# Chunked attention and top-1 experts on one core: PSUM banks of their own, loads beside the attention, a last round that leaves old slots in place

## The chip, the cores and the metric

The kernel runs on one core of a Trainium2 chip. The core has TensorE (PE: matrix products, and transposes by a product with the identity), VectorE (DVE), ScalarE (ACT), GpSimd (POOL), and SyncE (SP), which here only issues transfers. Sixteen DMA engines move data between the device memory (HBM) and the on-chip memory (SBUF). TensorE writes into PSUM, whose banks are read by VectorE and ScalarE. The metric is the device time of one execution in microseconds: 314.8 us for the kernel before, the median of three runs between 313.82 and 316.25.

## The reference

Two blocks in a row. The first is attention in chunks: 4 batches, 8 heads, 768 tokens, head dimension 64. A chunk of 32 queries sees 8 memory keys of its head and the keys from 16 before the chunk to 8 after it.

```python
scores = scale * np.matmul(q_c, k_full.transpose(0, 1, 3, 2))
a = np.exp(scores - np.max(scores, axis=-1, keepdims=True))
a = a / (np.sum(a, axis=-1, keepdims=True) + 1e-09)
out[:, :, c_start:c_end] = np.matmul(a, v_full)
```

The result, as 3072 tokens of 512 numbers, goes into eight experts. Each token goes to the one expert with the largest logit, and an expert keeps at most 80 tokens, those with the largest gate weight. A token that is kept becomes its gate weight times the expert's output; the others stay zero.

```python
logits = x @ w_gate                      # 3072 x 8
expert_idx = np.argmax(logits, axis=1)   # gate_w: its softmax probability
keep = np.argpartition(-gw, capacity)[:capacity]
h = np.maximum(x[tok_idx] @ w1[e], 0.0)  # 512 -> 1024
out[tok_idx] = gate_w[tok_idx, None] * (h @ w2[e])
```

All is in float32. One w1 or w2 matrix has 2.1 MB, and there are sixteen.

## The kernel before, in words

**Attention units.** The attention is cut into 32 units: a pair of heads, and half of a sequence (384 tokens). Four units make a round, which has all 512 features of 384 tokens; there are eight rounds. The loop over `i` (line 763) issues for each unit: `scores(i + 1)`, eight products in float32 on a mask product and two exponentials on ScalarE; the turns of a later k or q (`turn_k`, `turn_q`: GpSimd copies the loaded block into another order, TensorE transposes it, VectorE or ScalarE copies the result out of PSUM into `kT` or `qT`); `turn_x(i - 1)`, the transposes of the unit before's output; `values(i)` with `divide` on VectorE. It then issues the loads of k, q and v for later units. v's load is issued two units ahead, in rows of 64 numbers.

**Routing.** The class `Ranks` keeps a table of the best 80 tokens of each expert and merges each round into it. Its ten `steps` are spread over the four units of the next round, two in each unit, through the deque `later`. They weigh x with the gate matrix (`weigh`, `logits`), pick the expert (`gates`), count for each token how many of the round's tokens are ahead of it (`count`, `sum_counts`, `turn_counts`), compare it with the table's tokens (`rivals`, `older`), give everyone a slot (`slots`), and build the new table by products with one-hot matrices (`fill`). In `older`, the matrix `hoto` says which slot each old token moves to. The last round's steps have no later units to lie in: they follow the attention one by one (lines 810 to 843), and `place` makes from their result the token numbers that the gathers need.

**PSUM.** Four pools: `ps_t` with two buffers, shared by the turns of k and q, the turns of x and all steps of `Ranks`; `ps_s` with three for scores; `ps_o` with two for values; `ps_l` with one for the gate products.

**Experts.** `run_experts` gathers the 80 rows of an expert, turns them, multiplies with w1 (`up`, hidden tile hT), with w2 (`down`), turns back, scales and scatters the rows to the output. Nine matrices fit at once (`WR = 9`). w0, w1, the third (w2, in the tile `ld` that the q and k loads use until then), w3 and w4 have places of their own; w5 to w8 take the room of the attention's tiles. A later matrix is loaded by `load_next` in four pieces of 512 KB as soon as the one in its place has been used, and each piece waits until the third before it has landed. `busy` issues products of zeros that only keep TensorE working.

**The order of the transfers.** Nearly all are issued by SP, one after another, in the order of the program, and a transfer that waits for a buffer holds those behind it. The deque `slow` holds pieces that are not urgent: w0 and w1 in eight pieces, then `ld` in four. In the loop one is issued at every third unit from the ninth, and one at each of the last six. After the loop come w3 and w4, each whole, twelve transfers of zeros to the output (512 KB each), and w5 to w8, each whole. `in_order` fixes each engine's order as written.

Of the kernel before, what the change touches and what calls it, by code (L numbers as in the profile page):

```python
# [12 lines left out]
F32 = mybir.dt.float32  # L13
BF16 = mybir.dt.bfloat16
# [48 lines left out]
def kernel(  # L63
# [58 lines left out]
    behind = const.tile([128, 128 * (2 * NT - 1)], BF16, name="behind")  # L122
    iot = const.tile([128, cap], BF16, name="iot")
    iop = const.tile([cap, 1], F32, name="iop")
    idx_g = const.tile([cap, E], I32, name="idx_g")
# [24 lines left out]
    def busy(out, n, cols=DM // 2):  # L150

        for _ in range(n):
            nc.tensor.matmul(
                out[:, :cols], lhsT=zero[:, :128], rhs=zero[:, :cols], start=True, stop=True,
                skip_group_check=True,
            )

    class Weights:
# [32 lines left out]
    class Attention:  # L191
# [83 lines left out]

        def turn_q(self, n):
            if n >= NP:
                return
            qT = self.qT[n] = self.io.tile([128, S], F32, name="qT", tag="qT", bufs=5)

            qh = self.io.tile([NC, T0, 2, D], F32, name="qh", tag="turn", bufs=1)
            nc.gpsimd.tensor_copy(  # L282
                qh.rearrange("p t e d -> p e t d"), self.qs[n].rearrange("p e (t d) -> p e t d", d=D)
            )
            for t0 in range(0, T0, 4):
                pt = self.ps_t.tile([128, 4, NC], F32, name="pq", tag="t")
                for t in range(4):
                    nc.tensor.transpose(  # L288
                        pt[:, t, :], qh[:, t0 + t].rearrange("p e d -> p (e d)"), ident[:NC, :NC]
                    )  # L290
                nc.scalar.copy(  # L291
                    qT.rearrange("p (x t) -> p x t", t=T0)[:, :, t0 : t0 + 4], pt.rearrange("p t x -> p x t")
                )
# [75 lines left out]
    class Ranks:  # L369
# [3 lines left out]
        def __init__(self, gt, ps_t):  # L373
# [7 lines left out]
                mores=([32 * NT, HT], BF16), own=(full, F32), ahead=([128, NT], F32), slot=([128, NT], BF16),  # L381
                hot=([128, NT, cap], BF16), tab=([cap, ND, E], BF16), tabT=([3 * E, cap], BF16),
            )
# [92 lines left out]

        def older(self):

            over = self.ps("over")
            for i in range(NT):  # L480
                nc.tensor.matmul(
                    over[:cap, :E], lhsT=self.older_[:, i, :], rhs=self.oh[:, i, 0, :],
                    start=i == 0, stop=i == NT - 1,
                )
            nc.vector.tensor_reduce(self.beaten, self.older_, axis=AX, op=Alu.add)

# [86 lines left out]
        def steps(self, r, xTs, lu):  # L573
# [21 lines left out]
            ]  # L595

        def place(self, acc):

# [40 lines left out]
    with ExitStack() as actx:  # L639
        ps_t = actx.enter_context(tc.tile_pool(name="ps_t", bufs=2, space=PSUM))  # L640
        ps_s = actx.enter_context(tc.tile_pool(name="ps_s", bufs=3, space=PSUM))
        ps_o = actx.enter_context(tc.tile_pool(name="ps_o", bufs=2, space=PSUM))
        ps_l = actx.enter_context(tc.tile_pool(name="ps_l", bufs=1, space=PSUM))
        at = Attention(actx, ps_t, W.given[WR0])
# [36 lines left out]
        def for_slots():  # L681
            iot_i = gt.tile([128, cap], I32, name="iot_i")
            nc.gpsimd.iota(iot_i, pattern=[[1, cap]], base=1, channel_multiplier=0)
            nc.gpsimd.tensor_copy(iot, iot_i)
            iop_i = gt.tile([cap, 1], I32, name="iop_i")
            nc.gpsimd.iota(iop_i, pattern=[[0, 1]], base=1, channel_multiplier=1)
# [4 lines left out]

        slow = deque()
        for i in range(WR0):
            slow += W.load(i, 4)
        units = [(HP * b + c, f) for b in range(B) for f in range(2) for c in range(HP)]
        P, o, xr, xTs, lus = {}, {}, {}, {}, {}
# [31 lines left out]
        def turn_x(i):  # L728
            xTs[i] = at.turn_x(i, xr[i // HP], ps_t.tile([128, 512], F32, name="xt", tag="t"))

# [16 lines left out]
        later, done = deque(), deque()  # L747
        ranks = Ranks(gt, ps_t)
        start = len(list(nc.cur_bb.bb.instructions))
        busy(ps_o.tile([128, 512], F32, name="oy", tag="o"), 8)  # L750
        at.turn_k(0, nc.vector.tensor_copy)
        at.turn_q(0)
        at.turn_mem()
        at.put_mk(0)
        at.load_k(2)
# [7 lines left out]
        for i in range(NU):  # L763
# [4 lines left out]
            for kind, m in turns.get(i, []):  # L768
                (at.turn_k if kind == "k" else at.turn_q)(m)
            if i:  # L770
                turn_x(i - 1)
            if i in constants:
                constants[i]()
            if later:
                later.popleft()()
            values(i)
            if i and i % HP == 0:
                lus[r] = ps_l.tile([128, 512], F32, name="lu", tag="l")
                steps = ranks.steps(r - 1, [xTs[i - HP + c] for c in range(HP)], lus[r])
# [4 lines left out]
            if later:  # L784
                later.popleft()()
            for kind, m in turns.get(i, []):
                (at.load_k if kind == "k" else at.load_q)(m + 2)
# [6 lines left out]
            if i == NU - 6:  # L794
                slow += W.load(WR0, 4)
            if i >= NU - 6 or i >= 8 and i % 3 == 0:
                if slow:
                    slow.popleft()()
        turn_x(NU - 1)
        at.store(NR - 1, xr[NR - 1])  # L800
        for dma in slow:
            dma()
        for i in range(WR0 + 1, WR0 + 1 + WR2):
            for dma in W.load(i):
                dma()
        for dma in zeros():
            dma()


        r = NR - 1  # L810
        lp = ps_l.tile([128, 512], F32, name="lp", tag="l")

        nc.tensor.matmul(lp[:, : NT * E], lhsT=zerob, rhs=zerob[:, : NT * E], start=True, stop=False)
        early(range(HP - 1), lp)
        later.popleft()()
# [14 lines left out]
        for i in range(NT):  # L830
# [8 lines left out]
            if i == 1:  # L839
                ranks.older()  # L840
        ranks.slots(r, more)
        ranks.place(ranks.fill(r))
        busy(wait, 5)
        judge()
        in_order(start)

    def run_experts(ectx, tag, W, verdict=None, read_flag=None):
# [25 lines left out]

        pieces = deque()

        def load_next(i):

            if i < 2 * E:
                for dma in W.load(i, 4):
                    dma()  # L880
                    pieces.append(list(nc.cur_bb.bb.instructions)[-1])
                    if len(pieces) > 3:
                        tc.add_manual_dep(pieces[-1], pieces.popleft().name, follow, reason="pieces")

# [83 lines left out]
        turn_in(0)  # L968
        busy(ps_h.tile([128, 4 * cap], F32, name="wait", tag="hp"), 4)
        up(0)  # L970
# [17 lines left out]
    with ExitStack() as fctx:  # L988
        fw = fctx.enter_context(tc.tile_pool(name="fw", bufs=1, reuse_waits="tile"))
        W.pools[WR0 + 1 + WR2 :] = [fw] * (WR - WR0 - 1 - WR2)  # L990
        for i in range(WR0 + 1 + WR2, WR):
            for dma in W.load(i):
                dma()
        run_experts(fctx, "", W, verdict, read_flag)

    with tc.If(redo[1] > 0):  # L996

        with ExitStack() as actx:
# [12 lines left out]
            for i, (n, f) in enumerate((HP * b + c, f) for b in range(B) for f in range(2) for c in range(HP)):  # L1011
# [43 lines left out]
                if c == HP - 1:  # L1055
                    at.store(r, xr)
                    steps = ranks.steps(r, xTs, ps_l.tile([128, 512], F32, name="lu2", tag="l"))
                    for step in steps[: None if r < NR - 1 else 8]:
                        step()
            ranks.place(ranks.fill(NR - 1))  # L1060
        with ExitStack() as fctx:
# [34 lines left out]
```

## Time and profile before

The parts of the span (313.2 us), each row an answer of the trace for that stretch, times in us:

| stretch | what lies in it | PE busy | DVE | ACT | POOL | matmul clock | DMA share | GB/s |
|---|---|---|---|---|---|---|---|---|
| 0 to 20 | start, first units | 16.66 | 3.78 | 4.66 | 9.69 | 1.00, then 0.68 | 0.85, then 1.11 | 201, 232 |
| 20 to 60 | attention | 35.34 | 19.30 | 17.68 | 21.83 | 0.95 | 0.92 | 207 |
| 60 to 100 | attention | 35.19 | 20.27 | 18.13 | 17.62 | 0.91 | 0.83 | 184 |
| 100 to 140 | attention | 36.02 | 18.43 | 16.51 | 14.47 | 0.83 | 0.70 | 163 |
| 140 to 160 | attention | 17.45 | 10.92 | 8.94 | 5.32 | 1.00 | 0.68 | 170 |
| 220 to 240 | experts | 15.44 | 3.07 | 1.75 | 1.92 | 0.97 | 1.00 | 361 |
| 240 to 260 | experts | 19.10 | 2.17 | 1.31 | 3.80 | 0.94 | 0.97 | 309 |
| 260 to 280 | experts | 15.46 | 2.77 | 1.31 | 0.94 | 0.83 | 0.91 | 309 |

How to read it: "busy" counts each matmul from its start to its modelled end, so a busy TensorE is not one at its peak; the clock is the share of full speed granted to it. The DMA share is the time of the packets over 16 engines' time, and it can pass 1 since packets overlap; the GB/s beside it say what these packets carried. Over the whole span TensorE is busy 83%, VectorE 33%, ScalarE 26%, GpSimd 28%, and 70.44 MB move. The page's chain of work that ended last covers only the final scatters, so the stages have to be read from their own stretches.

In what follows, "unit 5" is the unit whose exponentials start at 37.77 us, unit 21 starts at 120.96 and unit 31 at 168.26. The last values product of the attention ends near 174, the first expert matmul starts at 200.39, and the last transpose of the experts ends near 301.5.

### The profile page before, as it was taken

How to read it: one execution, taken by the hardware profiler on the slowest of the kernel's cores; microseconds unless marked ns; L12 is line 12 of the kernel's file. 1: busy time of each engine (PE TensorE's matmuls, PEld its weight loads, DVE VectorE, ACT ScalarE, POOL GpSimd, SP SyncE). 2: the span in 40 equal slices, each digit the busy share in tenths (PEclk: the TensorE clock that was granted, in tenths of full speed). 3: DMA queues.
4: the chain of work that ended last, by engine and by line, in shares of the span. 5: the costliest groups of instructions: out<-in, count | busy, mean ns of one | idle time of the engine just before them, and what ended most of it. 6: DMA issues, size and time to landing. Idle time of an engine off the chain costs nothing. (4 is left out here: it accounts for less than half of the span.)

```text
span 313.2 us, 11255 instructions
## 1 busy us (share of the span) xinstructions
PE 258.4 (83%) x4982; PEld 219.8 (70%) x4982; DVE 103.3 (33%) x281; ACT 81.0 (26%) x196; POOL 88.1 (28%) x207
## 2 busy tenths in 40 slices
PE   8798898899889898888897777897797999499940
PEld 6677776677576776766775755786786988398830
DVE  1314337336366247264364364001101011010220
ACT  1234445424444334354454110010100101011000
POOL 3557518153173144260411013110012021010210
PEclk9859999969999759799999655799997999789985
DMA  7999995957959965817858499999998999993010
GB/s 190 230 229 222 195 228 121 268 122 160 270 119 284 226 152 152 180 36 211 197 153 277 138 378 390 375 322 365 395 386 278 349 279 305 307 312 117 25 38 16
DMA packets 63239, 70.44 MB, mean 225 GB/s; under 512 B 34621, under 2 KB 40797, under 8 KB 63181
## 3 DMA queue, kind: packets, MB, share of 16 engines
q1 hardware_dynamic: 61165, 66.65, 75.9%
q0 software_dynamic: 1056, 2.62, 2.4%
q8 instruction: 41, 0.67, 0.9%
q10 hardware_dynamic: 960, 0.36, 0.6%
q14 instruction: 17, 0.14, 0.2%
HBM read 55.72 MB, written 13.89 MB: 222 GB/s over the span
## 5 line engine op out<-in xcount | busy, mean ns | idle before, releaser
L897 PE MATMUL hp<-xn,w 128*64 128x80 f32 x896 | 37.0, 243 | 10.1 <-DMA w<-in_moe_w_dram 5.8
L897 PEld LDWEIGHTS hp<-xn,w 128*64 128x64 f32 x896 | 34.8, 145 | 12.3 <-DMA w<-in_moe_w_dram 6.6
L719 ACT ACTIVATE P<-sp 128x384 f32<-128x384 f32 x64 | 27.9, 488 | 44.3 <-PE sp L711 44.3
L711 PEld LDWEIGHTS sp<-qT,kT 64*128 64x128 f32 x512 | 36.7, 208 | 1.2 <-POOL kT L296 0.7
L711 PE MATMUL sp<-qT,kT 64*128 64x96 f32 x512 | 36.8, 289 | 0.5 <-POOL kT L296 0.4
L911 PE MATMUL yt<-hT,w 128*64 128x80 f32 x896 | 34.6, 239 | 0.9 <-issue 0.9
L911 PEld LDWEIGHTS yt<-hT,w 128*64 128x64 f32 x896 | 33.2, 142 | 2.4 <-issue 2.3
L901 ACT ACTIVATE hT<-hp 128x320 f32<-128x320 f32 x16 | 7.0, 437 | 98.0 <-PE hp L897 98.0
L333 PE MATMUL o<-vw,P 128*32 128x65 f32 x1536 | 32.1, 235 | 0.0
L959 POOL DMA_INDIRECT out_dram<-y,idx_s x7 | 6.5, 930 | 80.1 <-DVE y L958 60.6
L351 PE MATMUL xt<-ident,xr 128*128 128x128 f32 x96 | 18.4, 304 | 12.2 <-ACT qT L291 5.0
L322 DVE COPY kT<-pk 128x480 f32<-128x480 f32 x32 | 19.9, 654 | 24.0 <-PE pk L317 24.0
L333 PEld LDWEIGHTS o<-vw,P 128*32 128x32 f32 x1536 | 26.5, 117 | 1.4 <-issue 0.5
L429 POOL TENSOR_TENSOR desc<-oh,masks 128x24 bf16<-128x24 bf16 x16 | 3.3, 225 | 70.8 <-DVE over_s L340 34.7
L351 PEld LDWEIGHTS xt<-ident,xr 128*128 128x128 f32 x96 | 10.5, 147 | 17.6 <-ACT qT L291 6.9
L872 DVE COPY xn<-xp 128x320 f32<-128x320 f32 x8 | 3.9, 492 | 55.3 <-PE xp L870 55.3
L233 POOL COPY vw<-mv 8x512 f32<-8x512 f32 x32 | 20.0, 626 | 2.9 <-DMA mv<-in_mem_v_dram 2.9
L353 ACT COPY xT<-xt 128x384 f32<-128x384 f32 x32 | 15.4, 480 | 17.6 <-PE xt L351 17.5
L305 POOL COPY kh<-ld 96x1024 f32<-96x1024 f32 x15 | 15.5, 1033 | 12.5 <-issue 8.2
L282 POOL COPY qh<-ld 96x1024 f32<-96x1024 f32 x16 | 16.6, 1036 | 8.6 <-DMA ld<-in_q_dram 4.2
L288 PE MATMUL pq<-ident,qh 96*128 96x96 f32 x128 | 16.6, 270 | 2.8 <-DVE older__152 L472 1.5
L342 DVE TENSOR_TENSOR xr<-o,over_s 128x384 f32<-128x384 f32 x32 | 17.8, 557 | 1.1
(139 smaller groups left out, 337.5 us busy)
## 6 DMA issues: line engine op xcount, KB each, us to landing
w<-in_moe_w_dram SPq DMA_DIRECT2D x36, 512.0 KB, 6.1
w<-in_moe_w_dram SPq DMA_DIRECT2D x6, 2048.0 KB, 14.7
vw<-in_v_dram SPq DMA_DIRECT2D x60, 120.0 KB, 5.7
ld<-in_k_dram SPq DMA_DIRECT2D x16, 384.0 KB, 5.3
ld<-in_q_dram SPq DMA_DIRECT2D x16, 384.0 KB, 6.3
xd<-xr SPq DMA_DIRECT2D x8, 768.0 KB, 4.7
out_dram<-zero SPq DMA_DIRECT2D x12, 512.0 KB, 9.5
ld<-in_moe_w_dram SPq DMA_DIRECT2D x4, 512.0 KB, 7.1
```

Of the source, the lines that this page charges most:

```text
L233: nc.gpsimd.tensor_copy(vw[:MS, :, :, :D], self.mv[b][:, h : h + 2].unsqueeze(2).to_broadcast([MS, 2, NG, D]))
L282: nc.gpsimd.tensor_copy(qh.rearrange("p t e d -> p e t d"), self.qs[n].rearrange("p e (t d) -> p e t d", d=D))
L288: nc.tensor.transpose(pt[:, t, :], qh[:, t0 + t].rearrange("p e d -> p (e d)"), ident[:NC, :NC])
L305: spread(kh[:NC].rearrange("p t e d -> p e t d"), self.ks[n].rearrange("p e (t d) -> p e t d", d=D))
L322: nc.vector.tensor_copy(win[:, :, :, t0 : t0 + 4], _ap(pt, 0, [pt.ap[0], [JG, G], [1, (WK - MS) // T0], [NC, 4]]),)
L333: nc.tensor.matmul(out[32 * i : 32 * i + 32, e, t, :], lhsT=P[e][:, g, CHUNK * c : CHUNK * c + CHUNK], rhs=self.vw[n, f][:, e, g, :], star ...
L342: nc.vector.tensor_tensor(out=xr[:, :, 128 * c : 128 * c + 128].rearrange("p t (e d) -> p e t d", e=2), in0=o[:, :, :, :D], in1=over_s[:, ...
L351: nc.tensor.transpose(xt[:, 128 * t : 128 * t + 128], xr[:, t, 128 * c : 128 * c + 128], ident)
L711: nc.tensor.matmul(sp[e][:, g], lhsT=at.kT[n][r, NG * f + g, :], rhs=at.qT[n][r, HT * f + GQ * g : HT * f + GQ * g + GQ], start=False, sto ...
L719: nc.scalar.activation(P[i][e], sp[e], Act.Exp, scale=scale)
L897: nc.tensor.matmul(hp[j : j + 64, f, :], lhsT=w1[:, c, f1 : f1 + 64], rhs=xns[e][:, c, :], start=c == 0, stop=c == DK - 1,)
L911: nc.tensor.matmul(yt[j : j + 64, d, :], lhsT=w2[:, f, d * 128 + j : d * 128 + j + 64], rhs=hTs[e][:, f, :], start=f == 0, stop=f == FK - 1,)
```

## The change

- *PSUM.* `ps_l` goes, `ps_s` has two buffers for three, and a new pool `ps_x` has two, which serve the turns of x, the gate products and all steps of `Ranks`. `ps_t` is left to the turns of k, q and the memory keys, and to the last round's gate products `lp`. This is for turns and counting not to wait for each other's buffers. With it, the first step of a unit is issued ahead of `turn_x`.
- *Loads.* `slow` holds w0, w1, w3 and w4 (16 pieces), six of the twelve zeros, and later `ld`'s four. One is issued in each unit from unit 5. The other six zeros follow the attention, and these and w5 to w8, now in four pieces each, are issued like `load_next`'s: each waits for the third before it.
- *The last round.* An old token that stays in the table stays in its slot, and new tokens enter from slot `cap` downwards. `stay` computes who stays (`left`, `stays`), `enter` gives the new tokens their slots, `fill(0)` places only these, and VectorE adds the old table. `hoto` and its eight products are not needed there. Three of the four gate products of the last round are issued within units 30 and 31 (`early`).
- *Small things.* At the start the memory keys are turned ahead of q, the first q copy is split between GpSimd and ScalarE, and six for eight `busy` products are issued. The four ahead of `up(0)` go, and one of the five after `place`.

The diff, cut to its core (the branch for unusual inputs, line 996, is not run here):

```diff
+    pieces = deque()
+    def paced(dma):
+        dma()
+        pieces.append(list(nc.cur_bb.bb.instructions)[-1])
+        if len(pieces) > 3:
+            tc.add_manual_dep(pieces[-1], pieces.popleft().name, follow, reason="pieces")
...
-        def turn_q(self, n):
+        def turn_q(self, n, copies=(nc.gpsimd.tensor_copy,)):
...
+            for e, copy in enumerate(copies):
+                c = slice(0, 2) if len(copies) == 1 else slice(e, e + 1)
...
+        def stay(self):
+            over = self.over()
+            nc.vector.tensor_reduce(self.beaten, self.older_, axis=AX, op=Alu.add)
+            nc.vector.tensor_scalar(self.left, over[:cap, :E], iop, float(cap), op0=Alu.add, op1=Alu.is_le)
+            nc.gpsimd.tensor_tensor(
+                out=self.stays, in0=self.tab, in1=self.left.unsqueeze(1).to_broadcast([cap, ND, E]), op=Alu.mult
+            )
+        def enter(self, more):
...
+            nc.vector.tensor_reduce(self.ahead, self.own, axis=AX, op=Alu.add)
+            nc.vector.tensor_tensor(out=self.enters, in0=self.ahead, in1=self.beaten, op=Alu.is_lt)
...
+                nc.vector.scalar_tensor_tensor(
+                    out=self.slot, in0=self.ahead, scalar=-float(cap), in1=self.enters, op0=Alu.add, op1=Alu.mult
+                )
...
+                in1=iom.unsqueeze(1).to_broadcast(wide), op=Alu.is_equal,
...
+            acc = self.fill(0)
+            nc.vector.tensor_tensor(
+                out=self.held, in0=acc, in1=self.stays.rearrange("p i e -> p (i e)"), op=Alu.add
+            )
...
-        ps_s = actx.enter_context(tc.tile_pool(name="ps_s", bufs=3, space=PSUM))
+        ps_s = actx.enter_context(tc.tile_pool(name="ps_s", bufs=2, space=PSUM))
...
-        ps_l = actx.enter_context(tc.tile_pool(name="ps_l", bufs=1, space=PSUM))
+        ps_x = actx.enter_context(tc.tile_pool(name="ps_x", bufs=2, space=PSUM))
...
-        slow = deque()
+        slow, nothing = deque(), deque(zeros())
         for i in range(WR0):
             slow += W.load(i, 4)
+        for i in range(WR0 + 1, WR0 + 1 + WR2):
+            slow += W.load(i, 4)
+        for _ in range(6):
+            slow.append(nothing.popleft())
...
-        ranks = Ranks(gt, ps_t)
+        ranks = Ranks(gt, ps_x)
-        busy(ps_o.tile([128, 512], F32, name="oy", tag="o"), 8)
+        busy(ps_o.tile([128, 512], F32, name="oy", tag="o"), 6)
         at.turn_k(0, nc.vector.tensor_copy)
-        at.turn_q(0)
         at.turn_mem()
+        at.turn_q(0, (nc.gpsimd.tensor_copy, nc.scalar.copy))
...
-            if i:
-                turn_x(i - 1)
             if i in constants:
                 constants[i]()
             if later:
                 later.popleft()()
+            if i:
+                turn_x(i - 1)
             values(i)
...
+            if i == NU - 2:
+                lp = ps_t.tile([128, 512], F32, name="lp", tag="t")
+                nc.tensor.matmul(lp[:, : NT * E], lhsT=zerob, rhs=zerob[:, : NT * E], start=True, stop=False)
+                early([0, 1], lp)
+            if i == NU - 1:
+                early([2], lp)
...
-            if i >= NU - 6 or i >= 8 and i % 3 == 0:
-                if slow:
-                    slow.popleft()()
+            if i >= 5 and slow:
+                slow.popleft()()
...
-        for i in range(WR0 + 1, WR0 + 1 + WR2):
-            for dma in W.load(i):
-                dma()
-        for dma in zeros():
-            dma()
+        for dma in nothing:
+            paced(dma)
...
-        early(range(HP - 1), lp)
         later.popleft()()
         early([HP - 1], lp)
...
-                ranks.older()
-        ranks.slots(r, more)
-        ranks.place(ranks.fill(r))
-        busy(wait, 5)
+                ranks.stay()
+        ranks.place(ranks.enter(more))
+        busy(wait, 4)
...
-        busy(ps_h.tile([128, 4 * cap], F32, name="wait", tag="hp"), 4)
         up(0)
...
-            for dma in W.load(i):
-                dma()
+            for dma in W.load(i, 4):
+                paced(dma)
```

## The prediction

> **What bounds the kernel now.** I read four views: the slices of the span, the windows by stage, who TensorE waits for, and the order of its instructions. The slices come first.
>
> ```profile
> PEclk9859999969999759799999655799997999789985
> DMA  7999995957959965817858499999998999993010
> GB/s 190 230 229 222 195 228 121 268 122 160 270 119 284 226 152 152 180 36 211 197 153 277 138 378 390 375 322 365 395 386 278 349 279 305 307 312 117 25 38 16
> ```
>
> Each digit is 7.83 us. From slice 23 (180 us) to slice 35 (282 us) the DMA row stands at 9 and moves 280 to 395 GB/s. Before, it has holes (slices 16 to 18) and moves 120 to 280. I cut the span at the unit starts, where ScalarE's exponentials show them, and at the first and last expert matmul.
>
> ```profile
> core 0: us, PE busy (x) PEld busy (x) DVE busy (x) ACT busy (x) POOL busy (x), PEclk, DMA share, GB/s
> 37.80:121.00 83.20, 74.00 (x1383) 59.69 (x1383) 42.09 (x112) 36.75 (x91) 34.89 (x84) 0.90 0.82 189
> 121.00:168.30 47.30, 41.30 (x858) 33.25 (x856) 23.25 (x73) 21.00 (x55) 13.17 (x40) 0.96 0.69 177
> 174.00:200.40 26.40, 19.95 (x109) 15.65 (x106) 10.21 (x38) 2.04 (x6) 5.55 (x11) 0.57 0.95 337
> 200.40:301.50 101.10, 86.75 (x2110) 81.80 (x2109) 13.19 (x26) 6.99 (x16) 10.37 (x11) 0.94 0.82 279
> ```
>
> Units 5 to 21 (row 1) and the rest of the attention (row 2) keep TensorE 88% busy. The routing of the last round (row 3) is a chain with the matmul clock at 0.57. The experts (row 4) take 101.1 us; why 101 is in the order:
>
> ```profile
> 245.03 4.90 PE L897 MATMUL hp<-xn,w 128*64 128x80 f32 x128
> 255.21 0.58 PE L897 MATMUL hp<-xn,w 128*64 128x80 f32 x12
> 267.86 0.36 PE L897 MATMUL hp<-xn,w 128*64 128x80 f32 x4 [1.09 <-DMA w<-in_moe_w_dram]
> 272.19 6.25 PE L897 MATMUL hp<-xn,w 128*64 128x80 f32 x116 [1.65 <-DMA w<-in_moe_w_dram]
> ```
>
> One expert without a wait takes 255.21 - 245.03 = 10.2 us; others stand still for their weights. So the experts are bound by loads, the attention mostly by TensorE:
>
> ```profile
> PE xt L351 <- ACT qT L291: 5.0, 9, 0.6
> PE xt L351 <- DVE kT L322: 4.2, 10, 0.5
> PE lp L397 <- ACT xT L353: 2.9, 6, 0.8
> PE pq L288 <- DVE older__152 L472: 1.5, 3, 0.6
> ```
>
> These (20 to 174 us) are waits for a free bank: xt reads neither qT nor kT, pq does not read older. They name the shared two-buffer pool.
>
> **What the skill says.** The Trainium skill, PSUM — Partial Sum Buffer, Specifications, gives 8 banks per partition. Before, the pools take 2+3+2+1, after 2+2+2+2: the new pair is paid for with one scores bank and lu's. TensorE: Matmul & The Clock Gate, "The HAM clock gate", says the clock halves after an idle window of about 3.4 us and needs as long a busy one to return. The trace agrees on the levels: 0.50 at 14 to 22, 66 to 70, 106 to 116 and 176 to 194 us, after thin work. DMA: Bandwidth & Descriptors, "Queues, rings and completion order", says that rings are consumed in order: a weight piece issued ahead of a v load lies ahead of it. The trace shows v loads landing after 5.7 us (median), no case of a queue filled as after the change. Same page, "Why small descriptors are slow": the fixed cost per packet weighs on 256-byte ones. It agrees: full windows of the attention, with v's 256-byte rows, move about 230 GB/s at a share of 1.1; full windows of weights 385 to 420.
>
> **The change part by part.**
>
> *Loads moved.* Before, w0, w1 (8 pieces of 512 KB) and ld's four are issued beside the attention; w3, w4 and 12 zeros follow it. After, w3, w4 and six zeros go beside it too: 8+8+6+4 = 26 pieces, one per unit, i = 5 to 30. That takes 14 x 0.52 = 7.3 MB from behind the attention; at 360 GB/s (row of 210 to 240 us) 20 us less of loading there.
>
> Does it shorten the experts? Left behind the attention: 6 zeros and 11 matrices, 26.2 MB. Their issue is now paced three in flight, as the experts' pieces are; such a stretch (240 to 285 us) moved 306 GB/s, so 86 us. On TensorE's side: 101.1 less its waits there (hp on w 5.8, unexplained 4.3 + 1.6 + 0.9 = 12.6) less the loss by half clock after them (239 to 243 and 271 to 277 us, some 3) gives 85.5; 8 x 10.2 plus about 1 for the last expert's transposes gives 83. I take 84. Experts 0 and 1 and expert 2's w4 are resident at the start. With routing 22 us, the last matrix lands 86 us after the attention, and the product that reads it, which runs in the last 6 us, starts at 22 + 84 - 6 = 100. So weights are ahead by about 14 us and TensorE binds: -17. If the four pool-reusing matrices wait until routing frees the attention's tiles (15 us in), 15 + 23.1/0.306 = 90, still ahead.
>
> *The price in the attention.* Units 5 to 21 moved 15.7 MB, 4 pieces of it weights; now 16 pieces. DMA time: 0.82 x 83.2 = 68 share-us, less 4 x 1.4, plus 16 x 1.4 = 85; at the share of 1.1 that full windows reach, 77 us. TensorE's own floor: 74.0 busy, less half of the half-clock excess (64-72 and 105-116 us, some 8 lost) = 70. So here DMA becomes the bound at 77, against 83.2 now: -6. If full windows hold only 1.0, 85: +2. In the last units DMA has room (0.69 x 47.3 + 2 x 1.4 = 35 of 47); TensorE's 6.0 us of gaps lose some 4, clock 1: -5.
>
> *Banks and order.* xt, lu and counting get ps_x; kT/qT turns keep ps_t; later steps go ahead of turn_x. Per round of four units the gaps 0.41, 0.58, 0.43 and 0.5 go, and up to 0.35 comes back where xt waits for gp's copy in the same pool. That is the gain of about 2 us a round already counted above, as far as DMA lets it through. Two scores banks instead of three: exps end 1.0 us after the scores, the next scores come at least 1.4 later; cost nothing.
>
> *Start.* qh's 1.03 us copy on GpSimd, which holds shift and so the first pk, is halved with ScalarE; mem is turned first: -0.8. Units 0 to 4 save 1.5 of gaps.
>
> *Early products.* Nine of twelve (18 records, 3.99 us at half clock) leave the path between the last xt and lmax for units 30 and 31:
>
> ```profile
> 176.16 3.99 PE L735 MATMUL lp<-wgc,xT 128*128 128x8 f32 x18
> 186.89 0.82 DVE L490 TENSOR_TENSOR hoto<-iot,slo 80x640 bf16<-80x640 bf16 x1
> 197.34 3.12 PE L153 MATMUL wait<-zero 128*128 128x256 f32 x8
> ```
>
> lmax came at 181.54; with only the last three products, about 178.1: -3.4. In units 30 and 31 they cost some 1.2 us warm, in gaps there.
>
> *Slots left in place.* hoto (0.82) ahead of the last less goes, and with it eight small matmuls that were hidden. Added on VectorE: enters (0.2) and held (0.2, the row of a 128x24 operation) on the chain; left replaces slo; stays (0.2 to 0.4) and, once at the start, iom are on GpSimd beside other work. Behind held queues only place, which the first gather waits for. Sum -0.4, between -0.6 and +0.3.
>
> *Fillers.* Four matmuls of 256 columns ahead of up(0) go: they ran to 200.46 while xn was ready near 198.1: -2.2. They warmed the clock, so up(0) starts cold: +1.2 (0 to 2.5).
>
> Sum of the span: attention -0.8 -1.5 -6 -5 = -13, routing -3.4 -0.4 -2.2 +1.2 = -5, experts -17: 313.2 - 35 = 278. The time lies 1.7 above the span (314.95 and 313.2): **280 us**.
>
> **Rivals.** A is the above: 272 to 286, chance 0.52. B, DMA takes the pieces better than share times bytes says and TensorE binds throughout: units 5 to 21 take 70 rather than 77, and the half-clock stretches left go, -3: 270. For it: holes of 6 to 12 us in the DMA row. Against: nearly every hole follows a wait of the queue on a buffer, which stays. 0.13. C, the attention gains nothing, since every piece lies ahead of a v load that is needed two units later: 280 + 13 = 293. For it: DMA at 0.98 to 1.0 from 24 to 40 us already. 0.2. D, the paced issue binds the experts (the gap of three in flight, or a late first matrix): +6 to 10, 288. 0.07. E, slower: the queue's head-of-line wait starves values(i), TensorE idles and falls to half clock: 14 more pieces x 1.4 in series = 20, and half clock in ten units at 2 us each = 20, against 22 saved in routing and experts; with no gain elsewhere 315 + 40 - 22 = 333. Against it: SP issues v two units (9 us) ahead, against 5.7 to land. 0.05. No change within 1%: 0.03.
>
> **How the numbers follow.** The range 267 to 294 holds A, B, C and D but for their edges; it leaves out E, no change and the outer parts of B and C, under 2 in 10. Faster 0.92, same 0.03, slower 0.05.
>
> **What would show it.** Right: no line of TensorE waiting on w in the experts, their stretch 82 to 87 us, first expert matmul near 182; the waits of xt on qT and kT gone; DMA share near 1 through units 5 to 21 and their spacing 4.8 us; lmax 2.5 us after the last xt. Wrong: values waiting for vw loads, v landing over 9 us, more half-clock windows in the attention, or waits on w that remain.

## The result and the profile after

The changed kernel takes **300.84 us** (median of four runs, 298.36 to 302.87), the kernel before beside it 315.52. The ratio is 0.9525, with a 95% interval from 0.9431 to 0.962: about 15 us faster, where 35 were forecast (280 us, range 267 to 294). The forecast was wrong in size. Executions over 1.5% longer than a kernel's fastest are left out of the ratios, and five of the profiles below (the loads of before, v ahead, the fillers back, only the loads moved, two in flight) are of such ones, so a stage's time from them counts for much only where another profile bears it out. The profiled execution of the changed kernel took 298.36 us, its span is 296.3. The slices of the span, now 7.41 us each:

```profile
PEclk9555899999999755989999985559999999997996
DMA  7997999999999999999995819998889899992110
GB/s 193 238 231 159 192 240 246 223 284 199 217 292 214 236 303 214 211 290 252 321 279 148 271 66 347 333 338 305 313 303 312 298 278 317 332 319 110 29 34 21
```

The holes of the DMA row in the attention are filled: it stands at 9 from slice 4 to slice 20 (30 to 155 us, counted from 0). But up to slice 16 it moves mostly 200 to 250 GB/s. The windows cut at the same marks as before (units 5 to 21, 21 to 31, the routing, the experts):

```profile
core 0: us, PE busy (x) PEld busy (x) DVE busy (x) ACT busy (x) POOL busy (x), PEclk, DMA share, GB/s
39.49:123.36 83.87, 72.92 (x1383) 58.50 (x1383) 44.52 (x112) 36.28 (x91) 35.64 (x87) 0.90 1.12 242
123.36:168.22 44.86, 40.66 (x860) 32.83 (x859) 23.51 (x73) 20.99 (x54) 14.54 (x44) 0.96 0.95 260
174.60:194.11 19.51, 13.15 (x80) 9.79 (x73) 9.50 (x39) 2.04 (x6) 5.14 (x12) 0.51 0.93 307
194.11:288.57 94.46, 87.25 (x2109) 82.10 (x2109) 13.18 (x26) 7.00 (x16) 11.93 (x13) 0.96 0.75 252
```

| | before | after | forecast of the difference | measured |
|---|---|---|---|---|
| last values product ends | 174.0 | 174.6 | -13 | +0.6 |
| from there to the first expert matmul | 26.4 | 19.5 | -5 | -6.9 |
| experts | 101.1 | 94.5 | -17 | -6.6 |
| from the last expert matmul to the end | 11.7 | 7.7 | 0 | -4.0 |
| span | 313.2 | 296.3 | -35 | -16.9 |

So the attention gains nothing at all, the routing somewhat more than forecast, the experts a third of it. The last row was not forecast. At the end each scatter of rows waits for the one before it, and the seventh expert's landed sooner, before and after:

```profile
296.66 4.39 DMA out_dram<-y,idx_s
283.61 2.61 DMA out_dram<-y,idx_s
```

So the last scatter is issued 3.7 us behind the last expert product before and 1.7 after. The other 2 us lie behind that issue. The runs below take 7.4 to 9.7 us for this end with the changed code and 11.4 with the old routing; the cause was not tried.

TensorE's waits of 20 to 174 us show what the new banks did:

```profile
PE xt L364 <- DVE lg L420: 3.5, 6, 0.6
PE o L346 <- issue: 2.7, 2, 1.5
PE xt L364 <- ACT gbs L465: 2.5, 6, 0.7
PE o L346 <- DMA vw<-in_v_dram: 2.1, 3, 1.1
```

The waits of xt on qT and kT (9.2 us before) are gone. Smaller ones for the other users of the new pool (lg, gbs) came in their place. The second and fourth are new: the values product waits, by the fourth for v (the second names no cause). The order in time at one such place, and at the last expert's first products:

```profile
98.12 0.32 PE L346 MATMUL o<-vw,P 128*32 128x65 f32 x8 [1.06 <-DMA vw<-in_v_dram]
...
268.98 0.36 PE L944 MATMUL hp<-xn,w 128*64 128x80 f32 x4 [0.88 <-DMA w<-in_moe_w_dram]
270.30 5.87 PE L944 MATMUL hp<-xn,w 128*64 128x80 f32 x116 [0.97 <-SPq L1042]
```

After the first, the clock is at half from 100 to 117 us. v now takes a median of 10.5 us to land in units 5 to 21, where it took 6.1 before (first line before, second after):

```profile
vw<-in_v_dram SPq DMA_DIRECT2D x32, 120.0 KB, 6.1
vw<-in_v_dram SPq DMA_DIRECT2D x31, 120.0 KB, 10.5
```

### The profile page after: what moved, and what is told of

Its sections match the earlier page's. It is cut to its first block, busy times and chain, and to the rows that moved or that the text cites. A ratio compares the mean times of both kernels' runs of the same rounds, so it can differ in the third digit from the quotient of the medians.

```text
span 296.3 us, 11242 instructions
## 1 busy us (share of the span) xinstructions
PE 254.3 (86%) x4959; PEld 216.9 (73%) x4959; DVE 105.7 (36%) x282; ACT 81.0 (27%) x197; POOL 89.0 (30%) x209
## 5 line engine op out<-in xcount | busy, mean ns | idle before, releaser
L767 PEld LDWEIGHTS sp<-qT,kT 64*128 64x128 f32 x512 | 38.1, 213 | 1.4 <-POOL vw L243 0.6
L944 PEld LDWEIGHTS hp<-xn,w 128*64 128x64 f32 x896 | 36.1, 150 | 3.9 <-SPq L1042 1.1
L767 PE MATMUL sp<-qT,kT 64*128 64x96 f32 x512 | 38.2, 294 | 0.6 <-issue 0.3
L958 PEld LDWEIGHTS yt<-hT,w 128*64 128x64 f32 x896 | 32.5, 137 | 5.2 <-issue 5.0
L294 POOL COPY qh<-ld 96x1024 f32<-96x1024 f32 (+1 forms) x16 | 16.8, 1050 | 7.9 <-DMA ld<-in_q_dram 4.1
L301 PE MATMUL pq<-ident,qh 96*128 96x96 f32 x128 | 17.3, 290 | 0.6 <-DVE kT L335 0.6
L353 DVE RECIPROCAL over_s<-o 128x6 f32<-128x6 f32 x32 | 6.2, 193 | 32.2 <-PE o L346 32.2
## 6 DMA issues: line engine op xcount, KB each, us to landing
ld<-in_k_dram SPq DMA_DIRECT2D x16, 384.0 KB, 10.7
```

Source lines behind the costliest of these rows:

```text
L294: copy(qh.rearrange("p t e d -> p e t d")[:, c], self.qs[n].rearrange("p e (t d) -> p e t d", d=D)[:, c],)
L301: nc.tensor.transpose(pt[:, t, :], qh[:, t0 + t].rearrange("p e d -> p (e d)"), ident[:NC, :NC])
L767: nc.tensor.matmul(sp[e][:, g], lhsT=at.kT[n][r, NG * f + g, :], rhs=at.qT[n][r, HT * f + GQ * g : HT * f + GQ * g + GQ], start=False, sto ...
L944: nc.tensor.matmul(hp[j : j + 64, f, :], lhsT=w1[:, c, f1 : f1 + 64], rhs=xns[e][:, c, :], start=c == 0, stop=c == DK - 1,)
L958: nc.tensor.matmul(yt[j : j + 64, d, :], lhsT=w2[:, f, d * 128 + j : d * 128 + j + 64], rhs=hTs[e][:, f, :], start=f == 0, stop=f == FK - 1,)
```

## The experiments

The theory after this page, D: the banks do shorten the attention, by the 10 us or so that TensorE's floor allows, but the pieces of weights put beside it take the same time back, since the DMA engines were nearly full there, and give it back only in the experts. The rivals of D: P, the new banks only moved the waits and gave nothing; V, v comes late by its place in the queue and not by the rate, so that an earlier issue cures it; and for the experts F, three pieces in flight are too few. (These letters are not those of the forecast's rivals.)

**The loads of before in the kernel after.** `slow` is filled and emptied as before, w3 and w4, the zeros and w5 to w8 follow the attention unpaced:

```diff
-            if i >= 5 and slow:
-                slow.popleft()()
+            if i >= NU - 6 or i >= 8 and i % 3 == 0:
+                if slow:
+                    slow.popleft()()
...
```

> The changed kernel with the loads of before (pieces at every third unit, w3, w4 and all zeros behind the attention, w5 to w8 whole and unpaced); the banks, the order, the last round and the fillers stay as changed. Theory D (in the attention the DMA engines took back what the banks gave): units 5 to 21 fall from 83.9 us to 72 to 76, v lands in about 6 us again, the last values end near 167, and the experts go back to about 100 us. Theory P (the new banks only moved the waits and gave nothing): units 5 to 21 stay at 82 to 84 without the pieces too.

298.38 us (294.08 to 301.31), ratio 0.9382 with 0.9271 to 0.9494. Its windows, units 5 to 21 and the experts:

```profile
37.22:109.74 72.52, 65.79 (x1383) 52.78 (x1383) 43.42 (x112) 36.07 (x90) 35.88 (x87) 1.00 0.96 219
184.00:291.90 107.90, 90.66 (x2109) 84.69 (x2109) 13.17 (x26) 7.00 (x16) 11.87 (x13) 0.93 0.80 275
```

Units 5 to 21 take 72.5 us instead of 83.9, with v landing after 6.9 us and the clock at 1.00 throughout: the new banks and the new order give 10.7 us against the kernel before (83.2). A profile below with six pieces there (71.98) bears this out. The experts take 107.9 us in this execution instead of 94.5, with their weights coming later. By the whole times, whose intervals overlap, moving the loads on top of the banks is worth nothing that can be measured: the other parts of the change bring the whole gain without it. P falls.

**All pieces behind the attention**, read for units 5 to 21 alone:

```diff
-            if i >= 5 and slow:
-                slow.popleft()()
...
-        assert not slow
+        for dma in slow:
+            dma()
```

> All 26 pieces behind the attention, none beside it: only the attention is to be read. Theory D: units 5 to 21 at 70 to 73 us, no wait of a values product for v, v landing in 5 to 6 us. Theory P: 82 to 84 us. The whole is slower than the changed kernel by some 15 us, since 13.6 MB have to be loaded in front of the first expert matmul.

```profile
40.43:111.82 71.39, 64.81 (x1383) 52.57 (x1383) 43.42 (x112) 36.09 (x91) 35.90 (x87) 1.00 0.86 191
```

Without any piece the stage takes 71.4 us: with four, six or none it takes nearly the same, so this is TensorE's floor. The whole takes 321.01 us, since none of the 26 pieces is there when the attention ends. This run, the last and the kernel after price one piece in share-us, the DMA share times the length of the stretch: 0.86 x 71.39 = 61.4 with none, 0.96 x 72.52 = 69.6 with four, 1.12 x 83.87 = 93.9 with sixteen, so about 2.0 for each (the runs below give 1.8 to 1.9). The packets of the trace say the same: a piece has 128 packets of 4 KB or 256 of 2 KB, and in the kernel after one of 4 KB takes 253 ns on average in this stage, which is 128 x 0.253 / 16 = 2.0 share-us. In the kernel before, between 186 and 200 us, it takes 163 ns, which is 1.3.

**v three units ahead** instead of two, with a fifth buffer:

```diff
-name="vw", tag="vw", bufs=4
+name="vw", tag="vw", bufs=5
...
-            if i + 2 < NU:
-                at.load_v(*units[i + 2])
+            if i + 3 < NU:
+                at.load_v(*units[i + 3])
```

> v issued three units ahead with five buffers, for two with four. If the pieces hurt by latency (v lands after 10.5 us, two units are 10): the waits of values for v (7 us over the attention) go, the half clock after 100 us with them, units 5 to 21 at 76 to 78. If it is the rate of the DMA engines (241 GB/s in that mix): units 5 to 21 within 2 us of 83.9, v landing 4 us later than before.

302.62 us (298.38 to 307.86), ratio 0.9538 with 0.9415 to 0.9661: no gain.

```profile
41.09:123.41 82.32, 70.95 (x1383) 57.05 (x1383) 42.72 (x111) 36.10 (x91) 35.35 (x86) 0.92 1.11 233
```

The stage is 1.5 us shorter at nearly the same share, as the rate has it. But the edit does one thing more. GpSimd's copy of the memory's v rows into vw is issued a unit earlier too, and the load of these rows (`mv`) is not. The waits of 20 to 181 us:

```profile
POOL vw L243 <- DMA mv<-in_mem_v_dram: 28.6, 2, 15.1
PE pk L330 <- POOL kh L318: 8.5, 2, 6.3
```

The order of each engine is fixed, so k's copy stands behind that wait, and TensorE behind k's copy: 2.3 us in this stage, with the half clock from 89.6 to 96.4 us, and 6.3 us after it. In the kernel after no such wait of `pk` is listed. Without it the stage might have come near the 76 to 78 us that an effect of latency would give, so this run doesn't settle V. For the rate speaks a sum: at 1.14, the highest share of any 40 us in these twelve profiles, 93.9 share-us take 82 us. That is argued and not shown.

**The fillers back**: eight for six at the start, and the four ahead of `up(0)`.

```diff
-name="oy", tag="o"), 6)
+name="oy", tag="o"), 8)
...
         turn_in(0)
+        busy(ps_h.tile([128, 4 * cap], F32, name="wait", tag="hp"), 4)
         up(0)
```

> The six filler products removed (two at the start, four ahead of the first up) put back. If the gap of 2.1 us at the start brought the half clock early: half clock from about 13 to 23 us rather than 8 to 31, the third unit at 29.3 rather than 33.3. The first up takes 5.0 rather than 7.0 us but starts some 2.5 later: no gain there. If units 5 to 21 are bound by DMA, of the 4 us at the start less than half is left at the attention's end; if they are bound by TensorE, all of it.

301.53 us (298.93 to 307.17), ratio 0.9567 with 0.9456 to 0.9678: the same as the kernel after. The first `up` takes 4.84 us instead of 6.97, but 3.70 us of fillers stand before it: cold or warmed, it costs about the same. At the start, the fillers go with when the half clock begins: in the three profiles with eight of them (this one, the kernel before, only the loads moved) it begins at 13.1 to 13.6 us and lasts 10.2 to 13.7; in the nine with six it begins at 7.7 to 10.5 and lasts 17.0 to 27.3. The idle window of 3.4 us that the forecast names is not what is seen there: from TensorE's first product on, its longest pause before the half clock is 2.1 us in the kernel after, and inside it TensorE is busy 95% of the time. Unit 5 starts at 37.8 to 39.5 us with eight and at 37.2 to 41.5 with six, so what the two fillers are worth there stays open.

**The pieces spread by room**: the same 26 pieces, in six of the units 5 to 20 and two in each of 21 to 30.

```diff
-            if i >= 5 and slow:
-                slow.popleft()()
+            for _ in range(2 if i > 20 else i >= 5 and i % 3 == 2):
+                if slow:
+                    slow.popleft()()
```

> The changed kernel with the same 26 pieces at other units: one at units 5, 8, 11, 14, 17 and 20 (six where k, q and v load as well), two at each of units 21 to 30 (twenty, where only v and xd move). If the pieces cost time only where DMA is full: units 5 to 21 at 72 to 75 us rather than 83.9, the last ten units at 45 to 48, the last values near 163 to 165, the experts as changed (94), the whole at 288 to 292. If each piece costs its time wherever it lies: attention no shorter than the changed kernel's, 299 to 302.

**290.9 us** (287.6 to 291.99), ratio 0.9275 with 0.9188 to 0.9363. The kernel before scattered between 310.33 and 325.87 beside it, so the size of the gain is less sure than that, but all six runs lie below every run of the kernel after (298.36 and more).

```profile
40.48:112.46 71.98, 65.03 (x1383) 52.64 (x1383) 43.43 (x112) 36.11 (x90) 35.92 (x87) 1.00 1.00 227
112.46:162.03 49.57, 44.00 (x860) 35.47 (x859) 23.60 (x73) 21.00 (x54) 14.25 (x44) 0.90 1.04 290
...
190.92:281.46 90.54, 83.74 (x2109) 79.33 (x2109) 13.18 (x26) 7.00 (x16) 11.91 (x13) 0.98 0.77 257
```

Units 5 to 21 are back at the floor (71.98; two more profiles with this placing, below, show 72.95 and 71.76), and the last ten units pay 4.7 us (49.57 for 44.86) for ten pieces more. Their own traffic is only 0.47 of the DMA (114 GB/s in the run with all pieces last), so they have room, where units 5 to 21 with 0.86 have next to none. With sixteen pieces in units 5 to 21, the kernel after and three more profiles with its placing of the loads show 83.57 to 86.57.

**Only the loads moved**, in the kernel before, with the paced issue:

```diff
+        slow, nothing = deque(), deque(zeros())
...
+        for i in range(WR0 + 1, WR0 + 1 + WR2):
+            slow += W.load(i, 4)
+        for _ in range(6):
+            slow.append(nothing.popleft())
...
-            if i >= NU - 6 or i >= 8 and i % 3 == 0:
-                if slow:
-                    slow.popleft()()
+            if i >= 5 and slow:
+                slow.popleft()()
```

> The kernel before with only the new place and pace of the loads; banks, order, last round and fillers as before. If DMA's limit of about 84 us for units 5 to 21 and TensorE's 83 lie side by side (the larger binds): units 5 to 21 at 83 to 87, the experts 12 to 14 us shorter, the whole at 301 to 305. If the pieces cost their 11 us whatever TensorE does: 311 to 315.

313.88 us (307.26 to 315.19). Its runs are too few and too scattered for a ratio, and a gain of some us can't be excluded: the shortest, 307.26, lies below all of the kernel before beside it (310.33 to 325.87). The profile is of the longest run:

```profile
39.54:122.48 82.94, 70.39 (x1383) 56.35 (x1383) 41.94 (x112) 36.74 (x90) 34.58 (x84) 0.96 1.10 243
122.48:177.37 54.89, 45.94 (x858) 37.05 (x857) 23.26 (x73) 21.05 (x54) 13.16 (x40) 0.88 0.79 216
```

The experts shrink to 91.6 us, but units 21 to 31 take 54.9, where the kernel before has 47.3. That can't be put down to the loads: the run with the fillers back, whose code there is that of the kernel after (44.86), has 51.2. For units 5 to 21 the four profiles make a table:

| units 5 to 21, us | four pieces | sixteen pieces |
|---|---|---|
| old banks and order | 83.2 | 82.9 |
| new banks and order | 72.5 | 83.9 |

Only one field is short. The old banks hold the stage at 83 with the DMA share at 0.82, and sixteen pieces hold it there with the share at 1.10 to 1.12: two limits of nearly the same size, of which either is enough.

**Six pieces in flight** instead of three:

```diff
-        if len(pieces) > 3:
+        if len(pieces) > 6:
```

> The changed kernel with six pieces in flight for three. If three in flight hold the loads behind the attention to 276 GB/s: the last matrix lands near 255 rather than 269, the 3.9 us that the last up loses for its weights go, the experts at 88 to 90 us, the whole 4 to 6 us shorter. If the 16 engines are the limit: the same within 2 us, with gathers landing later.

300.71 us (299.92 to 305.49), ratio 0.9608 with 0.9509 to 0.9706: the same as the kernel after. Between 195 and 240 us the DMA carries 380 GB/s instead of 310. No product waits for weights any more, as F has it, and the experts still take 95.1 us. F falls as the account of the time. What takes the place of the waits is short stops of TensorE for which the trace names no cause ("issue"):

```profile
216.30 3.95 PE L944 MATMUL hp<-xn,w 128*64 128x80 f32 x107 [1.55 <-issue]
220.19 0.50 PE L923 MATMUL xp<-ident,xg 80*128 80x80 f32 x4
220.52 0.60 PE L1003 MATMUL yp<-ident,ys 128*80 128x128 f32 x4
221.26 0.16 PE L677 MATMUL kp<-okb,oneb 128*1 128x2 bf16 x1
221.36 0.63 PE L958 MATMUL yt<-hT,w 128*64 128x80 f32 x11
222.51 4.24 PE L958 MATMUL yt<-hT,w 128*64 128x80 f32 x117 [0.53 <-issue]
226.58 0.58 PE L944 MATMUL hp<-xn,w 128*64 128x80 f32 x11
228.98 4.24 PE L944 MATMUL hp<-xn,w 128*64 128x80 f32 x117 [1.83 <-issue]
```

Count the products from stop to stop: 107 + 4 + 4 + 1 + 11 = 127, then 117 + 11 = 128. Each has a weight load, so a stop comes after some 256 instructions. The page lists a queue of kind "instruction" with 41 packets and 0.67 MB, some 16 KB each. The Trainium skill, Runtime: NRT & Kernel Launch, "Instruction fetch mechanics", says that an engine's instructions are refilled in blocks of 16 KiB (256 instructions) by a DMA queue of its own, at a cost that is mostly hidden. The distance agrees; "mostly hidden" doesn't hold here, where the experts' eight stops sum to 10.0 us. This was theory I for the next runs: such a block waits behind the weight pieces.

The trace keeps the packets of that queue, and narrow windows find them. At 213.7 to 213.9, 220.1 to 220.3 and 226.3 to 226.5 us one starts in each:

```profile
q8 instruction: 1, 0.02, 34.6%
q8 instruction: 1, 0.02, 35.2%
q8 instruction: 1, 0.02, 34.2%
```

34.6% of 16 engines for 0.2 us is 1.1 us of one packet. They land near 214.9, 221.3 and 227.5, and the three stops listed above end at 216.30, 222.51 and 228.98: 1.2 to 1.5 us later each time.

**No loads of the last seven matrices**:

```diff
-            if i < 2 * E:
+            if i < 2 * E and len(W.pools) == WR:
+                W.t[i] = W.t[i - 8]
+            elif i < 2 * E:
                 for dma in W.load(i, 4):
                     paced(dma)
```

> The changed kernel without the loads of the last seven matrices: those experts use matrices that are already there, so the output is not the reference's; only the experts' time is to be read. If the 5.8 us that the down products lose in small gaps come from the loads beside them: experts at 84 to 87 us (the cold first up stays, 7 us). If they are TensorE's own: 90 to 92.

```profile
193.88:277.10 83.22, 81.46 (x2109) 78.20 (x2109) 13.18 (x26) 7.00 (x16) 11.92 (x13) 0.98 0.34 107
```

286.46 us, a single run. The experts take 83.2 us, with no stop for which no cause is named, and every `up` but the first in 4.60 to 4.65 us. So the forecast's floor of 84 was right, and what the kernel after takes beyond it, 94.46 - 83.22 = 11.2 us, goes with the loads beside the products, but for the 0.8 by which its cold first `up` is longer. Some 4.8 of it lie from the third-last `down` on, mostly in the last `up`, whose weights come late (8.65 us for 4.60). 5.7 lie between, where no product waits for weights. Of these, four stops at the ends of instruction blocks have 1.0 us idle, and six others, of 0.3 to 0.4 us in three `down`s, have 2.1.

**32 small products of zeros more**, while TensorE waits for the first gather, in the kernel with the pieces spread:

```diff
         busy(wait, 4)
+        for _ in range(32):
+            nc.tensor.matmul(
+                wait[:, : NT * E], lhsT=zerob, rhs=zerob[:, : NT * E], start=True, stop=True,
+                skip_group_check=True,
+            )
         judge()
```

> The kernel with the pieces spread, plus 32 small bf16 products of zeros on TensorE while it waits for the first gather. Theory I (TensorE's short stops in the experts are waits for the next 16 KB block of its instructions, which queues behind the weight pieces): the stops are tied to places in TensorE's stream, 127 to 128 products apart, so 32 more products ahead move every one of them 32 products earlier: the stop with 107 of 128 products left in the third up moves into the down before it with 11 left; those with 8 and 17 left in the sixth and seventh up move to 40 and 49 left; the time within 1% of 290.9. Rival R (the stops come from the data, a weight tile or a bank that the trace does not name): they stay at the same products of the same expert, 107, 8 and 17 left.

290.25 us (287.99 to 294.1): the time is the same, and the stops have moved. First the kernel with the pieces spread, then this one:

```profile
236.70 0.37 PE L924 MATMUL xp<-ident,xg 80*128 80x80 f32 x3 [1.66 <-issue]
258.47 0.84 PE L945 MATMUL hp<-xn,w 128*64 128x80 f32 x17 [0.55 <-issue]
```

```profile
231.80 1.32 PE L950 MATMUL hp<-xn,w 128*64 128x80 f32 x30 [0.34 <-issue]
253.36 1.94 PE L950 MATMUL hp<-xn,w 128*64 128x80 f32 x49 [1.04 <-issue]
```

The stop that had 17 products of the seventh `up` left has 49 left: 32 earlier. The one just after the fifth `up` (one xp product past it) now has 30 of it left: 31 earlier. None stayed. The stops that had 107 and 8 left have no successor 32 products earlier, since not every block is late. So the stops are tied to the instruction stream and not to data or banks, and R falls.

That they are waits for the blocks shows in the packets: the experts of the kernel before, of six in flight, of the kernel with the pieces spread and of this one have 25 stops of over 0.15 us without a named cause, and all 25 end 1.2 to 1.6 us after a 16 KB packet of the instruction queue has landed. So do five of the kernel after's eleven. How late the next packet starts goes with the loads: 3.7 to 4.5 us after a stop has ended with six in flight (all but the last stop), 2.1 to 3.4 with three (pieces spread), and there within 0.3 us of the block's place in the stream once all weights have landed. With six, some 3.8 + 1.1 + 1.4 = 6.3 us stand against the 4.65 in which 128 products run. That the engine asks for the next block just as it enters one is inferred.

**Two pieces in flight**, in the kernel with the pieces spread:

```diff
-        if len(pieces) > 3:
+        if len(pieces) > 2:
```

> The kernel with the pieces spread, two pieces in flight instead of three behind the attention. Theory I (the stops are instruction blocks that queue behind the pieces in flight): they shrink from 0.5 to 1.7 us to 0.3 to 0.8, and the experts go from 90.5 to about 88 if two in flight still carry the weights (1.05 MB per landing; 4 us to land would be 260 GB/s, where the experts need 23 MB in 90 us); the time 287 to 291. Rival L (two in flight carry less, since a landing costs a fixed time of about 3 us): 1.05 MB in 5 us is 210 GB/s, the last weights come late, waits on w return at the last two ups, the experts 95 or more and the time 295 to 302.

314.05 us (310.03 to 317.79), ratio 1.0034 with 0.9983 to 1.0085: the whole gain is lost.

```profile
PE hp L945 <- DMA w<-in_moe_w_dram: 22.3, 10, 6.2
```

One stop without a named cause is left in the experts (0.53 us), as theory I has it. But the DMA carries only 247 GB/s between 195 and 240 us, and the products wait 22.3 us for weights, more than rival L expected. So two and three in flight carry 247 and 313 GB/s in this kernel, and three and six 310 and 380 in the kernel after; a landing takes 4.2, 5.6 to 5.7 and 8.9 us. Two in flight lose the gain, and six gain nothing over three.

## Why the forecast was wrong, by its steps

- **"DMA becomes the bound at 77"**: units 5 to 21 took 83.9. The failed term is the price of a piece, taken as 1.4 share-us, near the rate of weights by themselves (1.3 in the kernel before, by packets). Among the attention's packets one costs about 2.0, by the packets too. 61.4 + 16 x 2.0 = 93.4, divided by the measured share of 1.12, is 83.4. That sum uses the same stage; with the runs of none and four pieces alone (2.05 for each) and the forecast's ceiling of 1.1 it gives 85.6. The base (68 less 5.6 = 62.4, measured 61.4), the ceiling (1.12) and the floor of 70 (71.4) stood. In the attention rival C's outcome came; whether by C's reason too, a v that lands late for its place in the queue, is not settled.
- **Banks and order**: right. They give 10.7 us in units 5 to 21 where the DMA lets them. The waits on qT and kT went as said, and with two scores banks for three the scores wait 0.3 us in all.
- **The last units, -5**: measured 44.86 for 47.30, -2.4. Their floor is 44.7, by the two runs with fewer pieces: the forecast took too much of their gaps for removable. Of pieces it counted two more there; the program has three more (ten for seven).
- **The start and units 0 to 4, -2.3**: measured +1.7 (unit 5 at 39.49 for 37.77). The two fillers that go at the start have no term in the forecast; with them goes a half clock that begins later and is shorter. With the start of the kernel after, the experiments show unit 5 between 37.22 and 41.46, so whether the change costs anything here stays open.
- **Routing, -5**: measured -6.9. From the last xt to lmax 6.15 became 2.93 (-3.2, said -3.4). From lmax to the first gather 9.40 became 9.06 (-0.3, said -0.4): the slots left in place are worth what two small additions and one removed hoto sum to. From the gather to the first `up` 9.45 became 6.38 (-3.1, said -2.2); 1.0 of this is a gather that landed sooner. The cold first `up`, counted here by the forecast, takes 6.97 for 5.09 (+1.9, said +1.2). Counted as the forecast counts, routing is right: -6.9 + 1.9 = -5.0.

```profile
177.19 1.45 PE L791 MATMUL lp<-wgc,xT 128*128 128x8 f32 x6 [0.51 <-ACT xT L366]
178.67 0.18 DVE L419 TENSOR_REDUCE lmax<-lp 128x3 f32<-128x24 f32 x1 [0.92 <-PE lp L791]
186.63 0.20 DVE L643 TENSOR_TENSOR held<-acc,stays 80x40 f32<-80x40 f32 x1 [0.55 <-PE acc L576]
```

- **"Weights are ahead by about 14 us and TensorE binds"**: -17 was forecast and -6.6 measured (-8.5 with the cold first `up` counted in the routing, as the forecast has it), by three errors. First, 306 GB/s was the rate of everything in such a stretch. All traffic runs at 310 here too, but the 44 pieces (23.07 MB) behind the attention take from 185.5 to 270.3 us, 272 GB/s; zeros, gathers, scatters and instructions share the rest. The last piece lands 96 us after the attention, not 86. Second, the forecast has the last matrix to land read in the last 6 us of the experts, 100 us after the attention. In the order of the program the last to land is the last expert's w1, since `up(3)` issues that expert's w2 first, and the last `up` starts at 267.5, 93 us after the attention. So the lead of 14 us was none. Third, the 6.8 us of unexplained stops of the kernel before (4.3 + 1.6 + 0.9) were counted as going away with its waits for weights. They are six stops like this one:

```profile
218.48 4.64 PE L897 MATMUL hp<-xn,w 128*64 128x80 f32 x127 [1.88 <-issue]
```

All six are waits at the ends of instruction blocks, by the packets. Such stops, and others without a cause, stay as long as pieces are loaded beside the products: 3.5 us of idle time in the kernel after. The floor of 84 was right (83.2).

- The forecast's rival D (the paced issue binds) comes near the sum in the experts, but a deeper issue didn't help. Its rival E (v starves TensorE, which falls to half clock) shows in part: the vw waits and the half clock from 100 to 117 us are its signs; they cost the attention the banks' gain, and no more.

Open are the two stops of 0.3 to 0.4 us in each of three `down`s of the kernel after, which lie at no fixed distance of products (they are gone without loads, and with the pieces spread), why a piece's packets take longer in the attention's mixture, and whether v's place in the queue has a part in the 83.9.

## What to carry to other kernels

Price a transfer that is to be moved at the rate of the stretch into which it goes, not at its own rate elsewhere, and look for the stretch with real room: here the same ten pieces cost 11.9 us in units 5 to 21 and 4.7 in the last ten units. When a change takes work off one engine in a stage and puts work on another there, undo each part alone: here the new banks bring 10.7 us in units 5 to 21, and the moved loads take it back, in a sum that looked like one gain. For a load that must come in time, look up when the program reads it, not only when the last one is read. In a stage full of products and loads, leave a few us for short stops that neither waits nor busy times name.

## What the runs showed of the hardware

- Beside loads TensorE stopped at places 127 to 128 products (some 256 instructions) apart, or a multiple of that, for 0.2 to 2.1 us. 32 products more ahead moved the stops by 31 to 32 products. Each of 25 ended 1.2 to 1.6 us after a 16 KB packet of the instruction queue had landed. Without loads there were none.
- Pieces of 512 KB with two and three in flight carried 247 and 313 GB/s in one kernel, with three and six 310 and 380 in another, all traffic together (195 to 240 us).
- The attention's mixture, v's rows of 256 bytes and sixteen weight pieces, moved 233 to 243 GB/s at a share of 1.10 to 1.12, with the new banks and with the old ones. A 4 KB packet took 253 ns on average there in the kernel after, and 163 ns between 186 and 200 us in the kernel before.
